# A batch's two small token tiles turned by half-row transposes in one step, and combine weights stacked four batches at a time

## The chip, the cores and the metric

The kernel runs on one core of one Trainium2 chip. The metric is the device time of one execution in microseconds (us), as the median of three runs. Beside it stands one execution that was taken with the hardware profiler; all rows below come from that execution, and their times count from the start of its span.

## What is computed

Attention with a learned position bias is followed by a soft mixture of experts. Inputs and outputs are float32.

```python
scores = q @ k.T / 8 + bias                    # B, H, S, D = 8, 8, 576, 64
attn   = softmax(scores) @ v
x      = attn.transpose(0, 2, 1, 3).reshape(4608, 512)
logits = x @ phi                               # 32 slots: 8 experts x 4
d = softmax(logits, axis=0)                    # over the 4608 tokens: dispatch
slot_input = d.T @ x                           # 32 x 512
slot_out   = relu(slot_input @ w1[e]) @ w2[e]  # per expert e, 512 -> 1024 -> 512
c = softmax(logits, axis=1)                    # over the 32 slots: combine
out = c @ slot_out                             # 4608 x 512
```

## The kernel before

The work is cut into 32 units: four pairs of heads (hp) times eight batches (b), unit u = 8 hp + b. A unit does the scores, softmax and value products of one pair of heads of one batch. Units 24 to 31 hold the last pair of heads, and each of them also does the mixture's work for its batch: `moe(u)` (line 566). A last stage then computes the slot outputs from streamed expert weights and combines them.

**The order of the work** is written out by hand in the string `ORDER` (line 24). A token `name/unit` is a step; a step emits its instructions on its engines at its place in the list, and every engine runs its own instructions strictly in that order. A `+` behind a token puts a copy on VectorE (DVE) instead of ScalarE (ACT). The steps that matter here, for a unit u and a row block p of its scores:

- `Sp.n` (line 417) computes scores on TensorE (PE) into two PSUM banks, `tp.hn` (line 442) adds the bias on DVE and thereby reads one of these banks, `ep.h` is the exponential on ACT, `mp` the reciprocal of the sums on DVE, `np.h` the scaling on GpSimd.
- `Tp`, `Rp` (lines 481, 515) turn the scaled rows by `half_turn` (line 403): one transpose of 64 rows by 128 columns, so that two row halves r = 0, 1 go to two different banks. `cp`, `cRp` (lines 501, 521) copy them out.
- `M0`, `M1`, `Mr` are the value products; `x0`, `x1` (line 556) copy their two banks into the token tile `xts`.
- `K01`, `K23`, `KR` (lines 592, 604) turn the tokens, `kc01`, `kc23`, `krc` copy them out; `L` (line 620) computes logits, `lc` copies them; `D` sums them over head groups; `d1`, `d2`, `dq`, `d3` (lines 649 to 706) take minima (DVE), exponentials into the tile `et2` (ACT), a copy of the logits into the tile `lq`, and the running state.
- `W` (line 720) turns `et2`, the dispatch weights, and `C` (line 731) turns `lq`, the combine logits: each by one 128 x 128 transpose and one of 32 x 128 (lines 712, 713), into one PSUM bank each. `wc` (line 723) copies the first into `ek`. `cA` (line 734) reads the second bank twice on DVE (a minimum over 32 slots, line 737, and a subtraction, line 738); `cB` and `cC` finish the softmax over slots in the tile `ck`. The last unit, 31, turns other tiles (line 716).
- `Z` (line 755) multiplies `ek` with the turned tokens on PE, `zc` (line 776) adds the result to a running sum on DVE.
- `A0`, `A1` (`stack`, line 1013) put the combine weights of four batches each into a pair of banks by 20 matmuls against an identity, and `Ac0`, `Ac1` (`stacked`, line 1027) copy them out. In the list they stand among the last steps of unit 31.

Then come `turn_slots` (line 974, its transpose is line 978), `first(j)` (line 986), the first expert product for j = 0 to 7, and the rest of the last stage; `refetch` issues the loads of later weights into tiles that `first(j)` has read.

**PSUM** has eight banks. `Banks(w, n)` (line 371) takes one bank or an aligned pair when a step is emitted, always the one that has been idle longest, and gives it back after the n-th `read()`:

```python
if w == 2:
    self.k = 2 * min((max(idle[2 * k], idle[2 * k + 1]), k) for k in range(4)
                     if 2 * k in idle and 2 * k + 1 in idle)[1]
```

So which earlier readers a step must wait for follows from the list alone. `T`, `R`, `K`, `L` and `Z` take pairs; `S` and `M0` take two single banks each.

Of the kernel before, what the change touches and what calls it, by code (L numbers as in the profile page):

```python
# [48 lines left out]
t1.11/2 S3.0/2+ t3.00/2 t3.10/2 lv/2 S2.0/2+ t2.10/2 e0.0/2 m0/2 n0.1/2 t2.00/2 S3.1/2+ t3.01/2 e1.0/2 t3.11/2 e1.1/2 w0/8 M0/1
S2.1/2+ S4.0/2 M1/1 m1/2 e3.0/2 t2.11/2 n0.0/2 t2.01/2 t4.10/2 e3.1/2 m3/2 e2.1/2 e2.0/2 t4.00/2 S4.1/2 t4.11/2 e4.1/2 m2/2 n1.1/2  # L50
n1.0/2 Mr/1 t4.01/2 x0/1 n3.0/2 n3.1/2 T3/2 e4.0/2 lv/3 x1/1+ R1/2 cR1/2 c3/2+ T0/2 c0/2 m4/2 S1.0/3 n2.1/2 t1.10/3 T1/2 n2.0/2
t1.00/3 c1/2 S1.1/3 n4.0/2 t1.11/3 T2/2 t1.01/3 c2/2 n4.1/2 e1.1/3 S0.0/3 S2.0/3 R3/2 t0.00/3 w1/10 t0.10/3 cR3/2+ T4/2 R4/2 cR4/2
t2.10/3 c4/2 t2.00/3 xs/1 S0.1/3+ e1.0/3 t0.01/3 t0.11/3 S3.0/3+ e0.1/3 e0.0/3 S2.1/3+ S3.1/3+ t2.11/3 e2.1/3 m1/3 t2.01/3 e2.0/3
xs/0 t3.10/3 n1.0/3 t3.00/3 M0/2 M1/2 n1.1/3 t3.11/3 m0/3 n0.1/3 t3.01/3 Mr/2 e3.0/3 m2/3 e3.1/3 x0/2 n0.0/3 R1/3 x1/2 cR1/3+ T0/3
m3/3 n2.1/3 n2.0/3 c0/3 lq/4 S1.0/4 T1/3 S1.1/4 t1.00/4 T2/3 t1.10/4 t1.11/4 c1/3 n3.0/3 t1.01/4 c2/3 S2.0/4 t2.10/4 t2.00/4
n3.1/3 T3/3 R3/3 cR3/3+ S0.0/4+ c3/3 e1.0/4 lq/5 S2.1/4+ lv/4 t0.10/4 e1.1/4 t0.00/4 S0.1/4+ t0.11/4 t0.01/4 m1/4 t2.11/4 e0.1/4
t2.01/4 S3.0/4+ t3.00/4 n1.0/4 t3.10/4 M0/3 e0.0/4 m0/4 n1.1/4 S4.0/4 S3.1/4+ t3.01/4 e2.1/4 e2.0/4 xs/2 e3.0/4 t3.11/4 m2/4
e3.1/4 M1/3 S4.1/4 t4.10/4 t4.11/4 e4.1/4 n0.1/4 Mr/3 t4.00/4 t4.01/4 x1/3 n2.1/4 m3/4 x0/3+ e4.0/4 n2.0/4 S1.0/5+ n0.0/4 R1/4
lv/5 cR1/4 t1.00/5 t1.10/5 T0/4 c0/4 S1.1/5 m4/4 t1.01/5 T1/4 n3.0/4 n3.1/4 c1/4 T2/4 t1.11/5 c2/4+ T3/4 c3/4 S0.0/5 n4.1/4 n4.0/4
T4/4 t0.00/5 R3/4 cR3/4 t0.10/5 S2.0/5 R4/4 cR4/4+ S3.0/5+ S0.1/5+ c4/4 M0/4 t2.10/5 t2.00/5 t3.10/5 S2.1/5+ t0.01/5 e1.0/5  # L60
# [155 lines left out]
def body(ctx, tc, qk, v, phi, mw1, mw2, tabh, consth, *outs):  # L216
# [349 lines left out]
    def moe(u):  # L566
# [138 lines left out]

        step(u, "d3", state)

        def turned(src, src2):
            h = Banks(1)
            pe = h.t  # L710
            if not fin:
# [467 lines left out]
```

## Time and profile before

| what | value |
|---|---|
| median of 3 runs | 539.65 us (539.45 to 541.40) |
| the profiled execution | 539.52 us, of which the span is 537.7 us |
| PE busy | 518.5 us, 96% of the span |
| DVE busy | 429.8 us, 80% |
| ACT busy | 459.1 us, 85% |
| GpSimd (POOL) busy | 223.2 us, 42% |
| DMA, mean over the span | 205 GB/s |

PE is TensorE's matmul stream and PEld its weight loads, which overlap it. A row of the timeline gives the start, the length, the engine, the line and operation, output <- inputs and a count; in brackets the idle time of the engine ahead of it and the instruction that ended this. Instructions of a helper carry the helper's line: 406 is `half_turn`, 360 every plain copy. In the chain of waits, a piece is a stretch in which one engine set the end of the program.

### The profile page before, as it was taken

To read this page: it belongs to the slowest core of one execution; us is meant where nothing else is said; L and a number is where in the kernel's file an instruction comes from. 1 tells how busy PE (TensorE), PEld (TensorE's weight loads), DVE (VectorE), ACT (ScalarE), POOL (GpSimd) and SP (SyncE) were. 2 spreads that over 40 slices of the span, in tenths; PEclk is the share of its full clock that TensorE was granted. 3 is DMA by queue.
4 is the path that set the end of the run, shared out by engine and by line. 5 is a ranking of instruction groups with operands and counts; after the bars stand their busy time and mean duration, and the time that the engine had idled before them with its cause. 6 is when DMAs were issued, how large, how long until landed. Compare 5 with 4: busy or idle time off the path is not lost.

```text
span 537.7 us, 22777 instructions
## 1 busy us (share of the span) xinstructions
PE 518.5 (96%) x9087; PEld 349.8 (65%) x9087; DVE 429.8 (80%) x1803; ACT 459.1 (85%) x988; POOL 223.2 (42%) x317
## 2 busy tenths in 40 slices
PE   8999899999989999999999999999999999999894
PEld 6444566767767676686776667666777667663661
DVE  6989878889879888889888888988899888761243
ACT  7998999999989999999999999999898898751132
POOL 4300655555454556565455556545234342300000
PEclk9999999999999999999999999999999999999997
DMA  6699535163963545576254638635632546999988
GB/s 217 245 313 351 169 108 196 47 209 115 281 190 117 189 129 173 172 243 221 68 188 138 211 129 260 171 115 195 231 98 69 172 130 219 322 354 378 406 324 328
DMA packets 40793, 110.14 MB, mean 205 GB/s; under 512 B 5360, under 2 KB 5488, under 8 KB 40688
## 3 DMA queue, kind: packets, MB, share of 16 engines
q1 hardware_dynamic: 40688, 108.70, 59.2%
q8 instruction: 71, 1.16, 0.9%
q14 instruction: 34, 0.28, 0.2%
HBM read 81.28 MB, written 27.41 MB: 202 GB/s over the span
## 4 chain that ended last, share of the span: by engine, by line
PE 81%; ACT 5%; DVE 5%; DMA 4%; issue 2%; POOL 1%; DVEq 0%; SPq 0%; ACTq 0%; POOLq 0%
PE ps L549 24%; PE ps L406 17%; PE ps L431 14%; PE ps L425 11%; PE ps L1041 3%; PE ps L993 3%; PE ps L1071 2%; PE ps L913 2%; DMA v<-in_v_dram 2%; DMA bias_m<-e 2%; DVE f L900 2%; PE ps L624 1%; ACT y L462 1%; DVE y L451 1%; ACT f L898 1%
## 5 line engine op out<-in xcount | busy, mean ns | idle before, releaser
L357 POOL TENSOR_SCALAR y<-y,rc 128x576 f32<-128x576 f32 x288 | 211.1, 750 | 219.1 <-DVE rc L470 171.6
L462 ACT ACTIVATE y<-y,mn 128x576 f32<-128x576 f32 x288 | 221.0, 776 | 7.9 <-DVE mn L451 6.8
L549 PE MATMUL ps<-at,v 64*64 64x288 f32 x2304 | 152.2, 403 | 2.1 <-DMA v<-in_v_dram 2.1
L360 ACT COPY at<-ps 128x1024 f32<-128x1024 f32 (+3 forms) x197 | 141.0, 759 | 10.3 <-PE ps L406 7.4
L451 DVE CUSTOM_DVE_ANT_0 y<-ps,bm 128x320 f32<-128x320 f32 x256 | 115.5, 487 | 10.5 <-PE ps L425 3.9
L549 PEld LDWEIGHTS ps<-at,v 64*64 64x64 f32 x2304 | 89.7, 133 | 49.2 <-DVE rc L470 2.7
L406 PEld LDWEIGHTS ps<-ident,y 64*128 64x128 f32 x2592 | 98.7, 138 | 32.8 <-POOL y L357 12.8
L451 DVE CUSTOM_DVE_ANT_0 y<-ps,bm,mn 128x256 f32<-128x256 f32 x256 | 113.9, 479 | 6.2 <-PE ps L425 1.1
L406 PE MATMUL ps<-ident,y 64*128 64x64 f32 x2592 | 106.6, 224 | 1.5 <-DVE mn L451 0.9
L431 PE MATMUL ps<-qk 64*64 64x256 f32 (+1 forms) x1280 | 92.9, 407 | 0.1
L425 PE MATMUL ps<-qk 64*128 64x320 f32 (+1 forms) x512 | 86.7, 431 | 1.3 <-DVE mn L451 1.2
L431 PEld LDWEIGHTS ps<-qk 64*64 64x64 f32 x1280 | 45.2, 132 | 28.7 <-ACT at L360 6.9
L462 ACT ACTIVATION_READ_ACCUMULATOR y<-y,mn 128x1 f32 x288 | 56.7, 197 | 0.0
L451 DVE DVE_READ_ACCUMULATOR2_ANT mn<- 128x1 f32 x576 | 48.3, 84 | 0.0
L425 PEld LDWEIGHTS ps<-qk 64*128 64x128 f32 x512 | 42.5, 189 | 7.3 <-DVE mn L451 3.0
L900 DVE TENSOR_SCALAR f<-tabw,offs 128x512 f32<-128x512 f32 (+17 forms) x107 | 39.9, 454 | 1.5 <-DMA bias_m<-e 1.4
L360 DVE COPY at<-ps 128x256 f32<-128x256 f32 (+3 forms) x59 | 34.5, 595 | 7.4 <-PE ps L406 6.4
L913 PE MATMUL ps<-f,wbd 128*32 128x512 f32 (+48 forms) x640 | 39.4, 390 | 0.5 <-ACT e L926 0.4
L913 PEld LDWEIGHTS ps<-f,wbd 128*32 128x32 f32 x640 | 18.3, 110 | 22.3 <-issue 10.2
L469 DVE TENSOR_REDUCE rc<-sm 128x2 f32<-128x4 f32 x144 | 22.0, 153 | 10.2 <-ACT y L462 9.8
L926 ACT ACTIVATE e<-ps,cons 128x591 f32<-128x591 f32 x35 | 26.7, 821 | 1.9 <-PE ps L913 1.9
L470 DVE RECIPROCAL rc<-rc 128x2 f32<-128x2 f32 x144 | 23.9, 166 | 5.0
(146 smaller groups left out, 404.6 us busy)
## 6 DMA issues: line engine op xcount, KB each, us to landing
wt<-in_moe_w_dram SPq DMA_DIRECT2D x62, 512.0 KB, 6.3
qk<-in_qk_dram SPq DMA_DIRECT2D x32, 576.0 KB, 4.1
bias_m<-e SPq DMA_DIRECT2D x32, 295.5 KB, 3.8
v<-in_v_dram SPq DMA_DIRECT2D x32, 288.0 KB, 3.3
bm<-bias_m SPq DMA_DIRECT2D x32, 288.0 KB, 4.9
out_dram<-ob SPq DMA_DIRECT2D x16, 512.0 KB, 4.5
xs<-xts SPq DMA_DIRECT2D x24, 288.0 KB, 4.3
xo<-xs SPq DMA_DIRECT2D x8, 864.0 KB, 4.7
```

The costliest lines, as they stand in the source:

```text
L357: nc.gpsimd.tensor_scalar(out=out, in0=y, scalar1=r, scalar2=1.0, op0=ALU.mult, op1=ALU.mult)
L360: (nc.vector.tensor_copy if eng else nc.scalar.copy)(out=out, in_=in_)
L406: nc.tensor.matmul(out, src[rs], ident[rs, rs], is_transpose=True, start=True, stop=True, tile_position=(64 * r, 0))
L425: nc.tensor.matmul(pss[hh].t[:, 0:nk], x[rs, S + p * P:S + (p + 1) * P], x[rs, ks], start=True, stop=True, tile_position=(64 * hh, 0))
L431: nc.tensor.matmul(pss[hh].t[64 * r:64 * r + 64, 0:nk], x[rs, q0:q0 + 64], x[rs, ks], start=True, stop=True, tile_position=(64 * hh, 64 * r))
L451: nc.vector.tensor_tensor_reduce(out=heads(hh)[:, cuts[n] // 64:cuts[n + 1] // 64], in0=d["ps", p, n][hh].read()[:, 0:nk].rearrange("a (k ...
L462: nc.scalar.activation(out=y, in_=y, func=AF.Exp, bias=d["mn", p][:, 2 + hh:3 + hh], scale=-1.0, accum_out=d["sm", p][:, hh, 0:1])
L470: nc.vector.reciprocal(out=r, in_=r)
L549: nc.tensor.matmul(d["po"][c].t[o:o + 64, 0:HALF], d["v"][rs, 64 * k:64 * k + 64], at[rs, c, 320 * k + start[c]:320 * k + start[c] + HALF] ...
L900: nc.vector.tensor_scalar(out=f, in0=tabw[:, 0:n], scalar1=off, scalar2=0.0, op0=ALU.add, op1=ALU.max)
L913: nc.tensor.matmul(x[32 * t:32 * t + 32, a:a + c1 - c0], wbd, y, start=True, stop=True, tile_position=(0, 32 * t))
L926: nc.scalar.activation(out=out, in_=x, func=AF.Copy, scale=invs[:, i:i + 1])
```

## The change

For units 24 to 30, `W` and `C` become one step, `W`: it takes a pair of banks and turns both tiles by eight half-row transposes; `wc` copies its part (now 192 elements wide, with 32 that nobody reads) and `cA` reads the other part, now by one minimum over six groups and two subtractions. The pair is given back after both readers. Unit 31 keeps its two steps.

`ck` is laid out so that the weights of four batches lie side by side, and `stack` turns them by nine half-row transposes in place of 20 matmuls. `stack` is called after the whole list, ahead of `turn_slots`, and `stacked` after `first(0)`. The host's reading of the output follows the new layout.

```diff
-    ck = const.tile([P, B, 5, 32], F32, name="ck")
+    ck = const.tile([P, 2, 5, 4, 32], F32, name="ck")
...
+        def both_turned(_):
+
+            h = m["W"] = m["C"] = Banks(2, 2)
+            for i, x in enumerate((et2, m["lq"])):
+                for j in range(2):
+                    for r in range(2):
+                        half_turn(h.t[:, r, 128 * i + 64 * j:128 * i + 64 * j + 64], x[:, P * j:P * j + P], r)
...
+            ek = xp.tile([P, 6, 32], F32, name="ek", tag="ek", bufs=2)
+            cp(eng, ek.rearrange("a (r c) s -> a r (c s)", r=2), x[:, :, 0:96])
+            m["ek"] = _Picked(ek, (0, 1, 3, 4, 2))
...
-        step(u, "W", weights)
+        step(u, "W", weights if fin else both_turned)
...
+            pk = x[:, :, 128:224].rearrange("a r (c s) -> a r c s", c=3)
+            km2 = km.rearrange("a (r c) -> a r c", r=2)
+            nc.vector.tensor_reduce(out=km2, in_=pk, axis=AX.X, op=ALU.min)
+            nc.vector.tensor_tensor(out=c_[:, 0:4].rearrange("a (r c) s -> a r c s", r=2), in0=pk[:, :, 0:2],
+                                    in1=km2[:, :, 0:2].unsqueeze(3).to_broadcast([P, 2, 2, 32]), op=ALU.subtract)
+            nc.vector.tensor_tensor(out=c_[:, 4:5], in0=pk[:, 0, 2:3], in1=km2[:, 0, 2:3].unsqueeze(2).to_broadcast([P, 1, 32]),
+                                    op=ALU.subtract)
...
-        step(u, "C", combine)
+        if fin:
+            step(u, "C", combine)
...
-        for i in range(4):
-            for j in range(4):
-                nc.tensor.matmul(h.t[32 * j:32 * j + 32, 0, i * P:(i + 1) * P], ck[:, 4 * q + i, j], ident, start=True,
-                                 stop=True, tile_position=(0, 32 * j))
...
+        for j in range(5):
+            for r in range(2 if j < 4 else 1):
+                half_turn(h.t[:, r, 64 * j:64 * j + 64], ck[:, q, j].rearrange("a b s -> a (b s)"), r)
...
             f()
+        stack(0)
+        stack(1)
         turn_slots()
         for j in range(4):
             first(j)
+            if j == 0:
+                stacked(0)
+                stacked(1)
```

In the order list only `W`, `wc`, `C`, `cA`, `A` and `Ac` move. The stretches, before and after (steps of other units between them are cut):

```
24 before: x0/25 T0/26 T1/26 n4.1/26 m2/26 cR1/26+ x1/25+ c1/26+ n4.0/26 W/24 e1.0/27 n2.0/26 C/24 cA/24 c0/26 L/25 wc/24 Z/24
24 after:  x0/25 T0/26 W/24 wc/24 cA/24 T1/26 n4.1/26 m2/26 cR1/26+ x1/25+ c1/26+ n4.0/26 e1.0/27 n2.0/26 c0/26 L/25 Z/24
25 before: x0/26 W/25 wc/25+ ... R1/27 w0/23 x1/26+ cR1/27+ n2.0/27 T1/27 c1/27 S0.0/28 ... m3/27 t0.00/28; far behind: C/25 ... cA/25
25 after:  x0/26 ... R1/27 W/25 wc/25+ cA/25 w0/23 x1/26+ cR1/27+ n2.0/27 T1/27 c1/27 S0.0/28 ... m3/27 t0.00/28
26 before: x0/27 n1.0/28 C/26 w0/21 ... W/26 e3.1/28 wc/26 ... t0.00/29 R1/28 cR1/28 T0/28 cA/26 cB/26 m3/28 ... t0.10/29 c0/28 S0.1/29
26 after:  x0/27 n1.0/28 w0/21 ... e3.1/28 ... t0.00/29 R1/28 W/26 wc/26 cR1/28 T0/28 cA/26 cB/26 m3/28 ... t0.10/29 c0/28 S0.1/29
27 before: d3/27 KR/27 lv/30 T1/29 n3.1/29 W/27 wc/27+ S4.0/30 S4.1/30 krc/27 Z/27; far behind: C/27 dq/28+ e1.0/30 cA/27
27 after:  d3/27 KR/27 lv/30 W/27 cA/27 T1/29 n3.1/29 wc/27+ S4.0/30 S4.1/30 krc/27 Z/27
28 before: W/28 wc/28 lc/29+ R1/30 cR1/30 lv/31 T1/30 D/29 C/28 c1/30 ... dq/29 ... d1/29 Z/28 cA/28
28 after:  lc/29+ R1/30 W/28 wc/28 cR1/30 lv/31 T1/30 D/29 c1/30 ... dq/29 ... d1/29 Z/28 cA/28
29 before: d2/29 W/29 zc/28 wc/29 ... K01/29 kc01/29 d3/29 KR/29 krc/29+ T2/30 c2/30 S1.1/31; far behind: C/29 ... D/30 cA/29
29 after:  d2/29 zc/28 ... K01/29 W/29 wc/29 cA/29 kc01/29 d3/29 KR/29 krc/29+ T2/30 c2/30 S1.1/31
30 before: M0/31 M1/31 Mr/31 J1/30 x1/31 W/30 kc23/30+ ... L/31 ... C/30 ... D/31 wc/30+ Z/30 dq/31 cA/30
30 after:  W/30 M0/31 M1/31 Mr/31 J1/30 x1/31 kc23/30+ ... L/31 ... D/31 wc/30+ Z/30 dq/31 cA/30
31 before: F2/30 F3/30 kc23/31 A0/31 krc/31 Z/31 zc/31 wxt/31 wxo/31 A1/31 Ac0/31 wxk/31 Ac1/31
31 after:  F2/30 F3/30 kc23/31 krc/31 Z/31 zc/31 wxt/31 wxo/31 wxk/31
```

## Rows read from the trace of the kernel before

**Rows 1.** The chain that ended last, by engine, share of the span.

```profile
PE 81%; ACT 5%; DVE 5%; DMA 4%; issue 2%; POOL 1%; DVEq 0%; SPq 0%; ACTq 0%; POOLq 0%
```

**Rows 2.** Stretches: length, busy PE PEld DVE ACT POOL, PEclk, DMA share, GB/s.

```profile
400.00:410.00 10.00, 9.97 (x172) 6.85 (x166) 9.41 (x44) 8.77 (x27) 5.74 (x8) 1.00 0.52 172
508.00:510.00 2.00, 0.67 (x16) 0.22 (x6) 0.00 (x0) 0.00 (x0) 0.00 (x0) 1.00 1.00 395
```

**Rows 3.** Pieces of the chain of waits: start, length, what.

```profile
374.48 0.26 PE ps L712
374.73 0.18 PE ps L713
...
437.15 0.32 DVE ck L738
...
464.97 0.26 PE ps L712
```

**Rows 4.** Timeline of the weight loads, half-row transposes R1/26, T0/26, T1/26.

```profile
373.14 1.20 PEld L406 LDWEIGHTS ps<-ident,y 64*128 64x128 f32 x36 [0.44 <-issue]
```

**Rows 5.** Groups by line and shape from 400 us on: count, busy us, mean ns, idle.

```profile
L738 DVE TENSOR_TENSOR ck<-ps,km 128x160 f32<-128x160 f32 x7 | 2.3, 325 | 0.2
...
L737 DVE TENSOR_REDUCE km<-ps 128x5 f32<-128x160 f32 x6 | 1.9, 317 | 0.0
```

**Rows 6.** Timeline around unit 29's d1: dq's copy on ACT, minima on DVE.

```profile
446.05 0.32 ACT L360 COPY lq<-ps 128x192 f32<-128x192 f32 x1
...
446.40 0.42 DVE L660 TENSOR_REDUCE mb<-ps 128x1 f32<-128x128 f32 x2 [1.05 <-ACT lq L360]
```

**Rows 7.** Timeline around unit 24's W: x0/25, x1/25, c1/26, L/25.

```profile
373.26 0.40 ACT L360 COPY xts<-ps 128x288 f32<-128x288 f32 x1 [0.44 <-PE ps L549]
...
373.86 0.45 DVE L360 COPY xts<-ps 128x288 f32<-128x288 f32 x1
...
374.59 1.23 DVE L360 COPY at<-ps 128x1024 f32<-128x1024 f32 x1 [0.27 <-PE ps L406]
...
375.27 0.12 PEld L624 LDWEIGHTS ps<-xo,phis 128*32 128x32 f32 x3
```

**Rows 8.** Timeline around unit 25's W: x1/26 on DVE, S0.0/28 and S0.1/28.

```profile
390.81 0.45 DVE L360 COPY xts<-ps 128x288 f32<-128x288 f32 x1
...
390.91 1.19 PE L425 MATMUL ps<-qk 64*128 64x320 f32 x8
```

**Rows 9.** Timeline around unit 26's W: wc/26, S0.1/29, t0.10/29.

```profile
407.64 0.27 ACT L360 COPY ek<-ps 128x160 f32<-128x160 f32 x1
...
407.99 0.68 PE L425 MATMUL ps<-qk 64*128 64x256 f32 x4
...
408.38 0.47 DVE L451 CUSTOM_DVE_ANT_0 y<-ps,bm 128x320 f32<-128x320 f32 x1
```

**Rows 10.** Timeline around unit 27's W: wc/27 and Z/27.

```profile
424.07 0.31 DVE L360 COPY ek<-ps 128x160 f32<-128x160 f32 x1
...
425.01 0.61 PEld L762 LDWEIGHTS ps<-xk,ek 128*32 128x32 f32 x16 [0.39 <-issue]
```

**Rows 11.** Timeline, units 28 to 31: lc/29, R1/30 with T1/30, krc/29, S0.1/31.

```profile
443.91 0.76 DVE L360 COPY lp<-ps 128x576 f32<-128x576 f32 x1 [0.21 <-PE ps L624]
...
444.21 0.70 PEld L406 LDWEIGHTS ps<-ident,y 64*128 64x128 f32 x20
...
449.45 1.40 DVE L360 COPY xk<-ps 128x512 f32<-128x512 f32 x2
...
450.90 0.70 PE L425 MATMUL ps<-qk 64*128 64x256 f32 x4
```

**Rows 12.** Timeline at the list's end: ACT's kc23/31 and krc/31.

```profile
478.39 2.11 ACT L360 COPY xk<-ps 128x1024 f32<-128x1024 f32 x3
```

**Rows 13.** Chain of waits at the list's end: A1, right ahead of turn_slots.

```profile
481.13 0.87 PE ps L1021 x32
482.00 0.26 PE ps L1024 x8
```

More of the change, by code (lines that the diff above doesn't have):

```diff
@@ L181 @@
[L181 to L184 removed]
+f12.2/-1 f15.0/-1 f9.2/-1 f15.3/-1+ f15.2/-1 f15.1/-1 B15/-1 f9.1/-1+ f12.1/-1+ f13.3/-1 f11.0/-1+ f13.0/-1 f11.2/-1
+f13.2/-1+ f11.3/-1+ f13.1/-1 f6.0/-1 f2.1/-1+ E15/-1 f11.1/-1 B13/-1 f12.3/-1+ f7.0/-1 B11/-1 f12.0/-1 B12/-1 f7.2/-1+
@@ L706, in moe, with turned @@
         step(u, "d3", state)
-        def turned(src, src2):
+        def turned(src):
             h = Banks(1)
-            pe = h.t
-            if not fin:
-                nc.tensor.transpose(out=pe[:, 0:P], in_=src2[:, 0:P], identity=ident)
-                nc.tensor.transpose(out=pe[:, P:P + 32], in_=src2[0:32, P:2 * P], identity=ident[0:32, 0:32])
-            else:
-                for cc in range(5):
-                    nc.tensor.transpose(out=pe[:, 32 * cc:32 * cc + 32], in_=src[0:32, cc * P:(cc + 1) * P],
-                                        identity=ident[0:32, 0:32])
-            return h
@@ L720, in weights @@
-        def weights(_):
-            m["W"] = turned(et, et2)
-        def keep_weights(eng):
-            m["ek"] = xp.tile([P, 5, 32], F32, name="ek", tag="ek", bufs=2)
-            cp(eng, m["ek"], m["W"].read()[:, 0:160].rearrange("a (c s) -> a c s", c=5))
-        step(u, "W", weights)
+            for cc in range(5):
+                nc.tensor.transpose(out=h.t[:, 32 * cc:32 * cc + 32], in_=src[0:32, cc * P:(cc + 1) * P],
+                                    identity=ident[0:32, 0:32])
+            return h
@@ L1018, in stack @@
         h = ends["H", q] = Banks(2)
-        for i in range(4):
-            for j in range(4):
-                nc.tensor.matmul(h.t[32 * j:32 * j + 32, 0, i * P:(i + 1) * P], ck[:, 4 * q + i, j], ident, start=True,
-                                 stop=True, tile_position=(0, 32 * j))
-        for i in range(4):
-            nc.tensor.matmul(h.t[32 * i:32 * i + 32, 1, 0:P], ck[:, 4 * q + i, 4, :], ident, start=True, stop=True,
-                             tile_position=(0, 32 * i))
+        for j in range(5):
+            for r in range(2 if j < 4 else 1):
+                half_turn(h.t[:, r, 64 * j:64 * j + 64], ck[:, q, j].rearrange("a b s -> a (b s)"), r)
     def stacked(q):
         h = ends["H", q].read()
-        nc.vector.tensor_copy(out=ends["cT", q], in_=h[:, 0].rearrange("a (b n) -> a b n", n=P))
-        nc.scalar.copy(out=ends["cR"][:, q], in_=h[:, 1, 0:64])
+        nc.vector.tensor_copy(out=ends["cT", q].rearrange("a j (r n) -> a r j n", r=2),
+                              in_=h[:, :, 0:256].rearrange("a r (j n) -> a r j n", j=4))
+        nc.scalar.copy(out=ends["cR"][:, q], in_=h[:, 0, 256:320])
     def second(k, Q, parts=(0, 1)):
@@ L1092, in body @@
     homes2 += [(wp, "w", (1024,)), (wp, "w", (1024,)), (wp, "w", (512,))]
-    for q in range(2):
-        step(U - 1, f"A{q}", lambda _, q=q: stack(q))
-        step(U - 1, f"Ac{q}", lambda _, q=q: stacked(q))
     with tc.manual_schedule():
@@ L1173 @@
     o = np.empty((8, 576, 512), np.float32)
-    o[:, 0:512] = main.reshape(4, 2, 2, 128, 2, 4, 128).transpose(1, 5, 2, 4, 6, 0, 3).reshape(8, 512, 512)
+    o[:, 0:512] = main.reshape(4, 2, 2, 128, 2, 4, 128).transpose(1, 2, 4, 5, 6, 0, 3).reshape(8, 512, 512)
     o[:, 512:] = rest.reshape(4, 128, 4, 2, 64).transpose(3, 2, 4, 0, 1).reshape(8, 64, 512)
```

361 lines of the change are left out of this document (195 added, 166 removed).

## Prediction

> **What bounds the kernel now.** I read the chain of waits first, then the busy time by stretch, then the timeline around each step that moves. The chain is PE for 81% of the span [rows 1]: look for a stretch in which PE never rests. In the mixture's stretch PE is busy 9.97 of 10 us and DVE 9.41 [rows 2]. DVE is a step behind PE, so work taken from PE pays only while DVE still hands back PSUM banks in time. Late in the last stage the picture turns: from 508 to 510 us PE is busy 0.67 of 2 us while the DMA share is 1.00 [rows 2]. [...]
>
> **The turns.** In each of seven batches a full transpose costs the chain 0.26 us and the small one 0.18, and both come twice: 0.88 us (the first two of four such pieces stand in [rows 3]). Half-row transposes come at 1.20/36 = 0.033 us each [rows 4], so eight cost 0.27 and a batch saves 0.61 us of PE, 4.3 us over seven. [...]
>
> **What is added.** `wc` copies 192 values in place of 160, about 0.03 us more. `cA` was 0.317 + 0.325 us [rows 5]. Its minimum now covers 192 values, between 0.32 and 0.38 (in proportion); the subtraction becomes two, together between 0.33 and 0.65. I take 0.35 + 0.50 = 0.85, in the middle, so 0.2 more on DVE in each batch. More important, two engines do not read one bank at the same time here: unit 29's minima on DVE need nothing from dq's copy but waited until it had ended at 446.37, and began at 446.40 [rows 6]. So `cA` also waits for `wc` where `wc` is on ACT and listed first (units 24, 26, 28, 29).
>
> **The pairs.** The new step holds a pair until both readers are done. I followed `Banks` through both lists, as the list alone fixes who takes which bank. The waits that this changes are the main cost.
>
> Unit 24: only one pair is idle when W/24 is emitted, and T1/26, the very next PE step, must take the same pair back. T0's last load ends at 373.14 + 20 x 0.033 = 373.8; x0/25 has freed the pair at 373.66 [rows 7]. W's loads end at 374.07. In the trace 0.25 us lie between the last load of T1 (374.34) and the start of its copy (374.59) [rows 4, 7], so `wc` starts at 374.3, `cA` at 374.65 and ends at 375.5. T1 started at 373.8 before and now at 375.5; its 16 loads end at 376.05. L/25, which started at 375.27 [rows 7], follows: 0.8 late with the saved turns already counted. It also needs x1/25, which ran at 373.86 on DVE and is now queued behind `cA`, behind m2/26 and cR1/26. PE holds L/25 and Z/24 behind it, ACT holds e1.0/27 and c0/26 behind `wc`. Bounds +0.7 (T1 alone, a shorter `cA`) and +1.3 (x1 late as well); I take **+1.0**.
>
> Unit 25: `cA` now stands ahead of x1/26 on DVE, which moves from 390.81 to 391.67 and ends at 392.1 [rows 8]. The second bank of S0.0/28 is now the one that x1/26 frees. S0.0 and S0.1 ran from 390.91 to 392.10, that bank's part from about 391.2. So PE loses some 0.75, and gains 0.44 when C/25 is not met later: **+0.3**, bounds 0 and +0.5.
>
> Unit 26: the second bank of S0.1/29 becomes the one that t0.10/29 frees, which stands behind `cA` and m3/28 on DVE. wc/26 ends near 407.95, `cA` at 408.8, then t0.10 takes 0.47: free between 409.3 and 409.5 [rows 9]. S0.1 ended at 408.67 and would now end near 409.7: **+1.0**, bounds +0.6 and +1.2. The saving is inside, as PE only waits longer.
>
> Unit 27: cA/27 moves ahead of wc/27, which goes from 424.07 to 424.9 [rows 10]. S4.1/30 takes `wc`'s bank for both halves, and Z/27 comes behind: about 0.7 late of 425.01. But `cA` leaves a place where DVE was the chain: 0.32 at 437 [rows 3] and most of the 0.317 of its minimum. **+0.1**, bounds -0.3 and +0.4.
>
> Units 28 and 29: T1/30 now takes lc/29's pair, free at 443.91 + 0.76 = 444.67, and ran from 444.35 (behind R1's four loads) [rows 11]: 0.3 late, and so D, dq and d1 of unit 29. On DVE come 0.2 more for cA/28 and 0.85 for cA/29, both ahead of krc/29. That moves from 449.45 by 1.35. S0.1/31 takes krc's banks and already started right at its end (450.85, started 450.90) [rows 11]. **+1.2**, bounds +0.6 and +1.4. Later C/29 leaves the chain: **-0.4**, the last piece of [rows 3] with the small one behind it.
>
> Unit 30: C/30 and W/30 stood where L/31 and D/31 waited for copies, so nothing is saved; W/30 is put ahead of M0/31, where PE has no gap: 0 to 0.27, I take **+0.2**.
>
> **The stacks.** A0 goes at no gain: Z/31 waits for krc/31, which ends at 478.39 + 2.11 = 480.50 on ACT [rows 12], and that covers it. A1 lies on the chain with 0.87 + 0.26 us [rows 13]; in its place come 18 half-row transposes, 0.59, partly beside zc/31. Bounds -0.4 and -1.1; I take **-0.6**. `stacked` costs nothing: its copies fall under first(1) to first(3), where DVE and ACT have no other work; without that cover they would be four copies on the path. Its banks go back before first(4) needs a new pair. The moved steps issue no DMA. GpSimd's memset of `lq` waits for the turn that read it and can only come earlier; the weight loads that SP issued between A0 and Ac1 wait for other tiles.
>
> **Sum.** 1.0 + 0.3 + 1.0 + 0.1 + 1.2 - 0.4 + 0.2 - 0.6 = +2.8 at first(0). The weights run at full DMA share behind it [rows 2], and their loads start as units 30 and 31 give up tiles, about +3.6 late by these terms; DMA was the later of the two at 508 us, so the end lies between +2.8 and +3.6. I keep +2.8, since PE reaches the weights earlier in this sum than the loads' shift says and the DMA gaps before can take the rest. On the profiled execution's own 539.52 us (span 537.7 and 1.8 around it) that is 542.3; the median of the runs lies 0.13 higher: 542.4.
>
> **Rivals.** First, faster: PE stays the bound and the pairs are there in time. [...] From rows: units 24 to 26 save 0.61 each, W/27 and W/28 0.17 each, C/29 0.4, the stacks 0.6, against 0.2 for W/30 and 0.3 for a longer `cA`: -2.5, 537.1 us. For it speaks PE's 81% [rows 1]; against it DVE's 9.41 of 10. The place that decides is T1/26: below about 0.6 us of wait there, the turn pays. Chance 0.20. Second, about half of the stalls: DVE and ACT work ahead while PE waits at unit 24, so units 25 and 28 to 29 lose little: +1.0, 540.6; chance 0.22. Third, the stalls add up and the weights' start carries the +3.6 and more to the end: +4, 543.6; chance 0.13. The forecast has 0.45. That the step itself fails to be shorter is hardly open, as rows 4 are the same instruction in the same alternation of halves.
>
> **Numbers.** 0.5%, 2.7 us, is about what a measurement of this kernel can tell from no change: the bounds are 536.9 and 542.4. The forecast has its middle at the upper one, so half of it, 0.23, and nearly all of the third rival, 0.13, are slower; a little of the second adds 0.01. Of the first rival under half is faster, 0.09. That leaves 0.54. The range of 537.3 to 543.9 leaves out half of the first rival and a third of the third, and some of the forecast's upper edge. The forecast's own range, with its bounds, is 541.2 to 543.6.
>
> **What would show it.** Right: an idle of PE or PEld of about 1.3 us before T1/26, ended by DVE `ck`; S0.0/28 ended by DVE `xts`; S0.1/29 and S0.1/31 ended by DVE; eight loads in 0.27 us at each turn; first(0) about 2.8 us later. Wrong: T1/26 without a wait, or a first(0) that comes no later than before.

## The result and the profile after

The changed kernel takes 547.44 us (median of 6 runs, 544.82 to 550.59), the kernel before 539.55 us (6 runs beside them, 538.22 to 541.40). The ratio is 1.0149 with a 95% interval of 1.0120 to 1.0177: 7.9 us slower. 542.4 was forecast, with a range up to 543.9; the direction was right, the size wrong.

The profiled execution took 549.96 us with a span of 548.2. Its page, part 1, and the chain of waits by engine, which answers to [rows 1]:

```profile
PE 522.4 (95%) x9053; PEld 353.3 (64%) x9053; DVE 431.2 (79%) x1810; ACT 459.1 (84%) x988; POOL 217.0 (40%) x317
...
PE 77%; ACT 7%; DVE 6%; DMA 5%; issue 3%; POOL 0%; SPq 0%; DVEq 0%; ACTq 0%; POOLq 0%
```

Every engine did nearly as much as before, but PE's share of the chain fell from 81% to 77%: it waits. Where, I read from landmarks that both kernels have, the starts of `L` in units 24 to 31 and of first(0). Their absolute times are of little use, since L/24, ahead of all that is changed, already started anywhere from 359.8 to 365.8 us in the profiles of this study. The stretches between them are very good: with the stacks alone changed, seven of eight repeat those of before within 0.01 us. So a stretch says what its unit costs, to a few hundredths, in one profile, where the granted clock is 1.00 in it and PE does not stand without a reason that the profile shows. Stretches of before, and the difference from them in each profile (us):

| stretch | before | changed | changed, again | stacks alone | W/30 old place | old turns, new order | units 25-29 | places | bank kept | units 26, 30 | halves |
|---|---|---|---|---|---|---|---|---|---|---|---|
| L/24-L/25 | 12.65 | +0.90 | +0.90 | -0.01 | +0.90 | +0.98 | -0.01 | -0.63 | +0.91 | -0.01 | -0.63 |
| L/25-L/26 | 17.74 | +1.32 | +5.39 | 0.00 | +2.59 | +1.18 | +1.17 | +0.60 | +2.32 | +0.01 | +0.15 |
| L/26-L/27 | 18.18 | +2.74 | +1.18 | +0.01 | +1.18 | +0.69 | +1.18 | +0.29 | +1.17 | +1.54 | +0.42 |
| L/27-L/28 | 19.40 | +0.72 | +0.73 | -0.01 | +0.73 | +0.58 | +0.73 | +0.70 | +0.73 | 0.00 | -0.01 |
| L/28-L/29 | 12.07 | -0.57 | -0.58 | -0.01 | -0.58 | -0.57 | -0.57 | +1.06 | -0.59 | -0.02 | 0.00 |
| L/29-L/30 | 19.20 | +0.83 | +0.82 | -0.01 | +0.84 | +0.72 | +0.83 | -0.86 | +0.83 | -0.01 | 0.00 |
| L/30-L/31 | 9.37 | +3.17 | +3.08 | +0.01 | +1.71 | +3.61 | +1.61 | +1.32 | +0.12 | +1.69 | +0.01 |
| L/31-first(0) | 11.60 | -0.27 | -0.28 | -0.49 | -0.49 | -0.28 | -0.49 | +0.96 | -0.50 | -0.29 | -0.49 |
| sum | 120.21 | +8.84 | +11.24 | -0.51 | +6.88 | +6.91 | +4.45 | +3.44 | +4.99 | +2.91 | -0.55 |

From first(0) to the end of the span it was 54.9 us before, 54.5 and 54.1 in the changed kernel: the end follows first(0). (In the other profiles it was 54.0 to 55.1, and 56.6 with the stacks alone.)

**Unit 24** in the changed kernel's timeline (the lines of [rows 4, 7]):

```profile
375.73 0.20 PEld L432 LDWEIGHTS ps<-ident,et 64*128 64x128 f32 x4
...
375.85 0.21 PEld L432 LDWEIGHTS ps<-ident,lq 64*128 64x128 f32 x4
...
376.24 0.32 ACT L386 COPY ek<-ps 128x192 f32<-128x192 f32 x1 [0.61 <-PE ps L432]
...
376.59 0.36 DVE L779 TENSOR_REDUCE km<-ps 128x6 f32<-128x192 f32 x1 [1.27 <-ACT ek L386]
376.99 0.29 DVE L780 TENSOR_TENSOR ck<-ps,km 128x128 f32<-128x128 f32 x1
...
377.19 0.18 DVE L782 TENSOR_TENSOR ck<-ps,km 128x32 f32<-128x32 f32 x1
...
377.52 0.71 PE L432 MATMUL ps<-ident,y 64*128 64x64 f32 x16 [1.32 <-DVE rc L495]
```

Read downwards, it is one pair of banks passing from hand to hand: eight half-row transposes in 0.33 us, `wc` on ACT, only then `cA` on DVE (idle 1.27 us, ended by `ek`), only then T1/26, which has stood for 1.32 us. (The releaser named there, `rc`, is the DVE instruction right behind `ck`.)

**Unit 26**, where two PE steps wait ([rows 9]):

```profile
411.63 0.71 PE L432 MATMUL ps<-ident,y 64*128 64x64 f32 x15 [0.50 <-DVE mn L477]
411.94 0.36 DVE L779 TENSOR_REDUCE km<-ps 128x6 f32<-128x192 f32 x1 [0.36 <-ACT ek L386]
...
413.43 0.48 PE L451 MATMUL ps<-qk 64*128 64x256 f32 x1 [0.67 <-DVE mn L477]
```

The second is S0.1/29, held by t0.10/29 behind `cA`, as forecast (with 0.67 us in place of 1.0). The first, T0/28, was not in the forecast: its pair is now one that t0.00/29 frees. Behind them the granted clock, in stretches of 1 us (columns as in [rows 2]):

```profile
413.00:414.00 1.00, 0.57 (x8) 0.46 (x9) 0.78 (x4) 0.99 (x2) 0.82 (x2) 1.00 0.00 0
414.00:415.00 1.00, 1.00 (x23) 1.00 (x22) 0.49 (x2) 0.02 (x1) 0.64 (x1) 0.53 0.06 16
415.00:416.00 1.00, 1.00 (x16) 1.00 (x14) 0.17 (x1) 1.00 (x2) 0.00 (x0) 0.50 0.00 0
416.00:417.00 1.00, 1.00 (x7) 0.99 (x6) 1.00 (x2) 1.00 (x3) 0.00 (x0) 0.50 0.00 0
```

0.50 is the lowest granted clock in this profile. PE works without a pause there, but slowly: from 415 to 417 us the 64 x 256 score matmuls took 683 ns each, against 393 ns between 396 and 412 us, at a clock of 1.00. That is 1.56 us of this stretch's +2.74; a second profile, with the clock at 1.00 here, has +1.18.

**Unit 30**, the largest loss, in the chain of waits and then by 1 us:

```profile
472.93 0.85 ACT at L386
473.78 0.06 issue
473.84 0.33 ACT lq L386
474.17 0.02 issue
474.20 0.43 DVE mb L686 x2
474.63 0.02 issue
474.65 0.17 DVE mb L688
474.82 0.02 issue
474.85 0.47 ACT et L702 x2
475.32 0.04 issue
475.36 0.28 PE ps L432 x2
...
476.24 5.86 PE ps L575 x72
```

```profile
474.00:475.00 1.00, 0.12 (x4) 0.00 (x0) 0.73 (x5) 0.81 (x4) 0.00 (x0) 1.00 1.03 339
475.00:476.00 1.00, 0.62 (x8) 0.48 (x8) 0.90 (x6) 0.69 (x5) 0.00 (x0) 0.75 1.04 401
476.00:477.00 1.00, 1.00 (x14) 0.60 (x14) 0.96 (x5) 0.00 (x0) 0.00 (x0) 0.50 0.97 347
477.00:478.00 1.00, 1.00 (x12) 0.49 (x8) 0.50 (x1) 0.00 (x0) 0.00 (x0) 0.50 1.06 405
```

The turn of W/30 reads `et2`, which d2/30 writes on ACT, at the end of a chain of five small steps; M0/31 stands behind it. The wait in the timeline:

```profile
475.36 0.66 PE L432 MATMUL ps<-ident,et 64*128 64x64 f32 x4 [1.24 <-ACT et L702]
```

In the kernel before M0/31 did not wait for that chain at all:

```profile
466.12 2.17 PE L549 MATMUL ps<-at,v 64*64 64x288 f32 x32
...
467.31 0.31 ACT L676 ACTIVATE et<-ps,mb 128x64 f32<-128x64 f32 x1
```

It ran from 466.12, 1.5 us before `et2` was complete. And in the changed kernel PE goes on at a granted clock of 0.50 right behind the wait: its 64 x 288 value products took 694 ns each from 476.3 to 478.5 us, against 407 in the kernel before from 466.2 to 468.5, and all 72 of them 5.93 us, against 4.59.

### The profile page after: what moved, and what is told of

Its sections match the earlier page's. It is cut to its first block, busy times and chain, and to the rows that moved or that the text cites. A ratio compares the mean times of both kernels' runs of the same rounds, so it can differ in the third digit from the quotient of the medians.

```text
span 548.2 us, 22722 instructions
## 1 busy us (share of the span) xinstructions
PE 522.4 (95%) x9053; PEld 353.3 (64%) x9053; DVE 431.2 (79%) x1810; ACT 459.1 (84%) x988; POOL 217.0 (40%) x317
## 4 chain that ended last, share of the span: by engine, by line
PE 77%; ACT 7%; DVE 6%; DMA 5%; issue 3%; POOL 0%; SPq 0%; DVEq 0%; ACTq 0%; POOLq 0%
PE ps L575 24%; PE ps L432 16%; PE ps L457 13%; PE ps L451 11%; PE ps L1084 3%; DMA bias_m<-e 3%; PE ps L1039 3%; PE ps L1114 2%; ACT y L488 2%; PE ps L650 2%; DVE y L477 2%; DMA v<-in_v_dram 2%; ACT e L972 1%; PE ps L279 1%; DVE f L946 1%
## 5 line engine op out<-in xcount | busy, mean ns | idle before, releaser
L575 PE MATMUL ps<-at,v 64*64 64x288 f32 x2304 | 153.8, 406 | 0.5 <-DMA v<-in_v_dram 0.5
L432 PEld LDWEIGHTS ps<-ident,y 64*128 64x128 f32 x2592 | 101.3, 139 | 38.2 <-POOL y L383 13.2
L575 PEld LDWEIGHTS ps<-at,v 64*64 64x64 f32 x2304 | 91.8, 134 | 47.0 <-ACT at L386 1.2
L432 PE MATMUL ps<-ident,y 64*128 64x64 f32 x2592 | 110.3, 226 | 4.5 <-DVE rc L495 1.8
L451 PE MATMUL ps<-qk 64*128 64x320 f32 (+1 forms) x512 | 89.2, 436 | 2.6 <-DVE mn L477 1.9
L451 PEld LDWEIGHTS ps<-qk 64*128 64x128 f32 x512 | 44.0, 191 | 9.4 <-DVE mn L477 3.9
```

The source lines that it names most:

```text
L432: nc.tensor.matmul(out, src[rs], ident[rs, rs], is_transpose=True, start=True, stop=True, tile_position=(64 * r, 0))
L451: nc.tensor.matmul(pss[hh].t[:, 0:nk], x[rs, S + p * P:S + (p + 1) * P], x[rs, ks], start=True, stop=True, tile_position=(64 * hh, 0))
L575: nc.tensor.matmul(d["po"][c].t[o:o + 64, 0:HALF], d["v"][rs, 64 * k:64 * k + 64], at[rs, c, 320 * k + start[c]:320 * k + start[c] + HALF] ...
```

## The experiments

There were eleven more runs: ten other kernels, and the changed one once more. Each is given against the kernel before in the same session, and by its column in the table above; where there is no column, the stretches are named. Of a kernel's edits, only the lines that matter are shown.

### The stacks alone

```diff
+JOINT = set()
...
-        step(u, "W", weights if fin else both_turned)
+        step(u, "W", both_turned if joint else weights)
...
-        if fin:
+        if not joint:
             step(u, "C", combine)
```

`joint` is true for the units in `JOINT`, here none. It runs with the turns and the order of the kernel before; `ck`, `stack` and `stacked` stay changed.

> The kernel before with the stacks alone changed (weights laid out by four batches, nine half-row transposes each, called behind the list); W and C as before, in their old places. If the stacks are the small gain that the changed kernel's trace shows between L/31 and first(0) (-0.27 us), all of L/25 to L/31 stand as before and the time is about 539.2 us, 0.3 below the kernel before. Rival: the weights' loads set the end and nothing changes, 539.5 us. Second rival: the stacks are part of the loss, because copies under the first expert products collide there; then 540.5 us or more.

540.23 us, ratio 1.0012 (0.9988 to 1.0037): no difference that can be measured. In the profile first(0) comes 0.51 earlier, all of it behind L/31. The stacks are a small gain and no part of the loss; the seven zeros of this column are what makes the table readable to a few hundredths. The gain does not reach the end of this profile, where it is 56.6 us from first(0) on in place of 54.9. PE waits there for nothing that the profile shows from 506.69 to 508.01, and then runs three microseconds at a granted clock of 0.50:

```profile
509.00:512.00 3.00, 3.00 (x58) 2.68 (x60) 1.22 (x1) 0.75 (x1) 0.00 (x0) 0.50 0.69 270
```

### W/30 back in its old place

```diff
-W/30 M0/31 M1/31 Mr/31 J1/30 x1/31 kc23/30+
+M0/31 M1/31 Mr/31 J1/30 x1/31 W/30 kc23/30+
```

> The changed kernel with W/30 alone put back behind x1/31, where it stood before; still one joint step. Theory: in its new place W/30 makes PE wait for the exponentials of d2/30 on ACT ahead of M0/31, and this wait is most of the +3.2 us between L/30 and L/31. Then that stretch falls back to within 0.7 us of before and the time to about 544.7 us. Rival: the stretch is long because ACT and DVE come late out of the earlier units; then it stays at +2.5 us or more and the time at 547 us.

545.60 us, ratio 1.0112 (1.0058 to 1.0166). L/30 to L/31 falls from 3.17 to 1.71 over before, so with the rest of the kernel as changed W/30's place is 1.4 of it; neither theory had the 1.7 that stay (the experiment with a bank kept says what they are). The clock tells what the 1.4 are: in this stretch 0.86 in both profiles of the changed kernel, and here

```profile
464.74:475.82 11.08, 9.75 (x183) 6.13 (x175) 5.68 (x17) 6.00 (x16) 1.49 (x3) 1.00 0.94 337
```

### The old turns in the new order

```diff
-x0/25 T0/26 W/24 wc/24 cA/24 T1/26
+x0/25 T0/26 W/24 C/24 wc/24 cA/24 T1/26
```

and so in all seven units; `W` and `C` are the old full turns into one bank each.

> The changed kernel's order of steps, with C right behind W, but the old turns (a full transpose and a small one each) into one bank each, given back after one reader. Theory one, the shared pair is the cause: T1/26 finds its pair at once, L/25 comes within 0.3 us of before, and L/27 within 1.5 us; the time is about 542 us, what is left being W/30's wait of about 2. Theory two, the order is the cause, because wc and cA now stand ahead of work of other units on ACT and DVE: L/25 is 0.5 us or more late, L/27 3.5 us or more, and the time 546 us or more.

546.75 us, ratio 1.0125 (1.0093 to 1.0156), first(0) +6.9. The time and L/25 (+0.98) are those of theory two, the order; L/27, with 0.98 + 1.18 + 0.69 = 2.85, lies between its 3.5 and the 1.5 of theory one. And its reason is not quite the one given. At unit 24 the list leaves one idle pair. W and C, as single banks, break it up, so T1/26 must wait for `cA` here as well: this run does not part the shared pair from the place at unit 24. At unit 26 the stretch pays 0.69 in place of 1.18. There W/26 waits for x1/27, and no other PE step by more than 0.3 us, where the changed kernel has the two waits of 0.50 and 0.67:

```profile
411.12 0.33 PE L741 MATMUL ps<-ident,et 128*128 128x128 f32 x1 [0.63 <-DVE xts L388]
```

The stretch of unit 30 again has a clock of 0.87.

### Units 25 to 29 only

```diff
+JOINT = {25, 26, 27, 28, 29}
...
-        step(u, "W", weights if fin else both_turned)
+        step(u, "W", both_turned if joint else weights)
```

Units 24 and 30 stand in the list as before, the others as changed.

> The changed kernel with units 24 and 30 put back to separate turns in their old places; the joint step in units 25 to 29 only. Theory one, the lateness of ACT and DVE after unit 24's stall is carried on into units 25 and 26: without it L/27 comes about +2.0 us late in place of +5.0 (so less than the 0.9 of unit 24 alone would explain), and the time is about 541.5 us. Theory two, each unit pays its own wait whatever went before: L/27 at +4.1 us and the time 547.4 - 0.9 - 3.2 = 543.3 us.

543.52 us, ratio 1.0069 (1.0042 to 1.0096). The time is theory two's. L/24 to L/27 loses 2.34, between the 2.0 of theory one and the 4.1 of theory two; but the 4.1 had in it the 1.56 us of lowered clock of the first profile, and 2.5 are left without them. Stretch by stretch it is plain: 1.17 and 1.18 here, and 1.32 and, at a clock of 1.00, 1.18 where unit 24 is stalled as well. Each unit pays its own wait. L/30 to L/31 still loses 1.61, with unit 30 as before: the first sign that its place is not the whole cause.

### The changed kernel once more

> The changed kernel once more, for a second profile. Where the granted clock fell in the first (0.92 of full speed between L/26 and L/27, 0.86 between L/30 and L/31) two theories differ. If the fall follows from this kernel's own waits, both stretches are again some 1.5 us longer than the waits alone make them (20.9 and 12.5 us) with the clock at about 0.9. If it is chance of one execution, the clock is 1.00 there and the stretches are 19.4 and about 11.1 us.

One execution, 551.92 us. Between L/30 and L/31 the clock is 0.86 again and the stretch 12.45: the fall came in both executions, as the first theory has it. Between L/26 and L/27 the clock is 1.00 and the stretch 19.36, as the second has it: the first fall there belonged to that execution. A new stall stands between L/25 and L/26:

```profile
385.80 0.80 PE L432 MATMUL ps<-ident,y 64*128 64x64 f32 x11 [2.62 <-issue]
```

with the clock at 0.93 behind it. "Issue" means that PE waited for nothing that the profile shows. The same stall, behind the same sixth load of the same sixteen, is there with W/30 in its old place (1.25 us) and with the bank kept (next, 0.97 us), not in the first profile.

### A bank kept from C/29 to D/30

```diff
-T2/31 c2/31 D/30 dq/30
+T2/31 G/29 c2/31 D/30 g/29 dq/30
+        if u == 29:
+            step(u, "G", lambda _: m.update(G=Banks(1)))
+            step(u, "g", lambda _: m["G"].read())
```

W/30 is in its old place too.

> The changed kernel with W/30 in its old place, and in addition one PSUM bank is taken where C/29 stood and given back behind D/30, with no instruction in between. With that M0/31 finds the two banks of c2/31, as in the kernel before, in place of one that d2/30 reads last. Theory: the +1.7 us that are left between L/30 and L/31 with W/30 in its old place are M0/31's wait for d2/30 through this bank, a consequence of C/29 having left; they go, and C/29's saved turn shows: that stretch is at -0.4 us against before (9.0 us), the time about 543.5 us. Rival: ACT and DVE come late into this stretch (cA/29 and krc/29 moved) and M0/31 would wait anyway; then it stays above 10.5 us.

544.50 us, ratio 1.0116 (1.0076 to 1.0156). L/30 to L/31 falls from +1.71 to +0.12:

```profile
467.38:476.87 9.49, 9.07 (x183) 5.96 (x175) 5.67 (x17) 5.98 (x16) 1.48 (x3) 1.00 0.98 341
```

No instruction was added. A bank that C/29 used to hold had steered M0/31 to the two banks of c2/31; without C/29 it gets D/30's, and waits for d2/30. That is shown for W/30 in its old place. The saved turn of C/29 (-0.4) did not appear on top. In the kernel before, C/29's turn ran at 464.90 while the next PE step, R3/31, had to wait for a pair that a DVE copy frees; without C/29 PE rests there instead. Before, and with the bank kept:

```profile
464.58 1.23 DVE L360 COPY at<-ps 128x1024 f32<-128x1024 f32 x1 [1.61 <-PE ps L406]
464.90 0.33 PE L712 MATMUL ps<-ident,lq 128*128 128x128 f32 x1
...
465.86 0.34 PE L406 MATMUL ps<-ident,y 64*128 64x64 f32 x4
```

```profile
471.37 0.34 PE L433 MATMUL ps<-ident,y 64*128 64x64 f32 x4 [0.42 <-DVE at L387]
```

### Units 26 and 30 only

```diff
+JOINT = {26, 30}
```

> The kernel before with the stacks, and the joint step in its new place in units 26 and 30 alone; the other units as before. Two questions, read from two stretches. Unit 26: if the units price their waits one by one, L/26 to L/27 pays the +1.2 us that it paid with units 25 to 29 changed, less the 0.4 that C/25, back in its old place, costs there either way: +1.2 to +1.6 us. If that price was lateness handed on by unit 25, it is +0.5 us or less. Unit 30: if W/30 ahead of M0/31 is enough by itself to make PE rest and the granted clock fall, L/30 to L/31 is +3 us with a granted clock near 0.86; if it takes the lateness of units 28 and 29 as well, the clock stays 1.00 and the stretch is at +1.7 us or less. Time 544 us by the first theories, 541 us by the rivals.

543.37 us, ratio 1.0056 (1.0023 to 1.0089). Unit 26 pays +1.54 with nothing late ahead of it; with C/25 still there (0.44 by the forecast, not measured alone) that is 1.1 to 1.2 net, the first theory. The waits themselves are others here: 0.51 us of W/26 for x1/27 and 0.74 of S0.1/29, none of T0/28, so the equal sum is partly chance. Unit 30 pays +1.69 with the clock at 1.00: W/30 makes PE wait 1.27 us for `et2`, but that rest alone did not bring the clock down. C/29 is in its old place in this kernel. By the list, W/30 takes the pair of c2/31 ahead of M0/31, so M0/31 gets D/30's bank here too.

```profile
462.33:473.39 11.06, 9.77 (x184) 6.32 (x177) 5.85 (x18) 5.64 (x15) 1.55 (x3) 1.00 0.91 336
```

### The joint step in roomier places

```diff
-x0/25 T0/26 W/24 wc/24 cA/24 T1/26 n4.1/26 m2/26 cR1/26+ x1/25+ c1/26+ n4.0/26 e1.0/27 n2.0/26 c0/26 L/25 Z/24
+x0/25 T0/26 T1/26 n4.1/26 m2/26 cR1/26+ x1/25+ c1/26+ n4.0/26 e1.0/27 n2.0/26 c0/26 W/24 wc/24 cA/24 L/25 Z/24
...
-R1/27 W/25 wc/25+ cA/25 w0/23 x1/26+ cR1/27+ n2.0/27 T1/27
+R1/27 w0/23 x1/26+ cR1/27+ W/25 wc/25+ cA/25 n2.0/27 T1/27
```

and alike in the other five units.

> The changed kernel's joint step and its stacks, with W, wc and cA of all seven units moved to places where the list leaves a pair idle for some time and the banks taken behind it were given back long before (unit 24: behind T1/26, ahead of L/25; 25: behind x1/26 and cR1/27; 26: behind x1/27; 27: behind x0/28; 28: ahead of S0.0/31; 29: ahead of K23/29; 30: ahead of D/31). Theory: the loss comes from the places, not from the joint step, so the waits go and PE's saving shows: L/24 to L/25 -0.6, the two stretches behind it -0.6 each, L/27 to first(0) together -1 or so; first(0) about 2.8 us earlier than before and the time near 537 us. Rival: the step itself is dear (the readers of one pair follow each other, cA is longer on DVE); then L/24 to L/27 stays at +1.5 us or more over before and the time at 541 us or more.

541.89 us, ratio 1.0028 (1.0005 to 1.0051): the theory's 537 failed. The rival's time came, but not its stretch: L/24 to L/27 is at +0.26, not at +1.5. Unit 24 gives -0.63, to a few hundredths PE's saving:

```profile
377.43 0.20 PEld L433 LDWEIGHTS ps<-ident,et 64*128 64x128 f32 x4
...
377.56 0.20 PEld L433 LDWEIGHTS ps<-ident,lq 64*128 64x128 f32 x4
...
377.83 0.12 PEld L651 LDWEIGHTS ps<-xo,phis 128*32 128x32 f32 x3
```

`L` follows 0.4 us behind the first turn and nobody waits. In the other units I chose places by how long ago the banks had been given back in the list, and that was not enough: the rest of the sum is +4.1. Of these some 1.45 are a lowered clock between L/31 and first(0) (+0.96 in place of -0.49), ahead of which PE had rested no more than in kernels without a fall there:

```profile
476.90:489.46 12.56, 11.44 (x192) 8.24 (x191) 8.98 (x34) 6.84 (x17) 0.00 (x0) 0.86 0.90 329
```

The others are waits. At unit 30, +1.32, M0/31 waits for d2/30. At unit 26 PE still stands 1.20 us, behind `x1/27` and `cA` on DVE; unit 28's step stands one stretch earlier than in the changed kernel, and the two have +1.06 and -0.86. That a bank has long been free does not say that its next reader is.

### Half-row transposes without the joint step

```diff
+            h = Banks(2)
+            for j in range(2):
+                for r in range(2):
+                    half_turn(h.t[:, r, 64 * j:64 * j + 64], src[:, P * j:P * j + P], r)
```

for W/26 and C/30 in their old places, with one reader each; unit 24 alone has the joint step.

> The kernel before with the stacks, the joint step in unit 24 alone, behind T1/26 and with wc and cA ahead of c0/26; and W/26 and C/30 by four half-row transposes into a pair of their own, given back after one reader, in their old places. Theory: half-row transposes are worth their 0.3 us (one tile) and 0.6 us (two) on PE where the pair they take was idle and nobody waits for it: L/24 to L/25 -0.6 us, L/25 to L/26 within 0.1 of before, L/26 to L/27 -0.3, first(0) about 1.4 us earlier than before, the time 538 to 539 us if the end follows first(0), 539.6 us if the loads of the expert weights set the end. Rival: a wider pair costs a later step as much as the turn saves; then first(0) is not earlier than with the stacks alone (-0.5 us).

539.67 us, ratio 1.0000 (0.9977 to 1.0023). -0.63 at unit 24 as expected, +0.15 behind it where 0.1 was the most expected; W/26 has +0.42 for the expected -0.3, and first(0) comes 0.55 earlier, not 1.4. T0/28 now takes the pair that wc/26 frees:

```profile
406.59 0.71 PE L435 MATMUL ps<-ident,y 64*128 64x64 f32 x16 [0.40 <-ACT ek L389]
```

A wider turn is itself a consumer of pairs: the rival, at this place.

### Unit 24 alone, twice

Both are the kernel before with the stacks and this one stretch of the list changed, first:

```diff
-cR1/26+ x1/25+ c1/26+ n4.0/26 W/24 e1.0/27 n2.0/26 C/24 cA/24 c0/26 L/25 wc/24 Z/24
+cR1/26+ x1/25+ W/24 wc/24+ c1/26+ n4.0/26 e1.0/27 n2.0/26 cA/24 c0/26 L/25 Z/24
```

> What the runs so far point to: the kernel before with the stacks, and the joint step in unit 24 alone, behind T1/26, with wc on DVE ahead of c1/26 and cA ahead of c0/26. L/24 to L/25 -0.6 us, the stretch behind it within 0.1 us of before (with wc on ACT, Z/24 came 0.1 late there), the others as before, L/31 to first(0) -0.5: first(0) 1.1 us earlier. If the end follows first(0), the time is 538.5 us, 0.2% below before, about as much as five rounds can tell; if the weights' loads set the end, it is no different from before. Rival: wc on DVE makes c1/26 late, and the stretch behind L/25 gives the 0.6 back.

538.39 us, ratio 0.9973 (0.9952 to 0.9994). -0.63, then +0.50, the rival: Z/24 takes the pair of c1/26, which is late on DVE behind `wc`.

```profile
376.87 1.09 PE L816 MATMUL ps<-xk,ek 128*32 128x256 f32 x16 [0.48 <-DVE at L388]
```

and second:

```diff
+cR1/26+ x1/25+ c1/26+ n4.0/26 W/24 e1.0/27 n2.0/26 wc/24 cA/24 c0/26 L/25 Z/24
```

> The kernel before with the stacks and the joint step in unit 24 alone, this time with wc on ACT, as in the run with the halves, ahead of c0/26 (there the stretch behind L/25 lost 0.15 us; with wc on DVE it lost 0.50, because c1/26, whose pair Z/24 takes, came behind wc). Expected: L/24 to L/25 -0.63, the next stretch +0.15, the others 0, L/31 to first(0) -0.49: first(0) 0.97 us earlier than before and 0.3 earlier than with wc on DVE; the time 538.2 us, 0.3% below before. Rival: the end does not follow first(0), and the time is no different from before, 539.8 us.

538.36 us, ratio 0.9961 (0.9944 to 0.9978). Every stretch came as written within 0.01 us: -0.63, +0.15, five zeros, -0.49, first(0) 0.98 earlier. It is faster than the kernel before by 0.4% (the interval is 1.2 to 3.0 us, and the stretches account for 1.0 of them), and by some 1.8% than the changed one, measured in another session (0.9961 against 1.0149). In these runs the change pays in one unit of seven, in another place than it was put, and in the stacks.

## Why the prediction was wrong, step by step

**The parts were priced right.** Eight half-row transposes take 0.33 us (0.27 forecast), and where nothing waits a batch saves 0.63 (0.61). `cA` takes 0.36 + 0.29 + 0.18 = 0.83 (0.85). `cA` waits for `wc` where both are on one pair: in the group by line its minimum has 1.6 us of idle time ended by `ek`.

**Unit 24**, +1.0: 0.90, by the mechanism named. The point from which the first rival would have won, a wait of T1/26 below 0.6, was passed with 1.32.

**Unit 25**, +0.75 up to L/26: 1.32, and 1.17 with unit 24 as before. The wait of S0.0/28 for x1/26 is there; T1/27 stands besides, since its pair now contains a bank that t1.11/28 frees late. In the kernel with units 25 to 29 only:

```profile
393.57 0.51 PEld L433 LDWEIGHTS ps<-ident,y 64*128 64x128 f32 x14 [0.20 <-DVE mn L478]
...
394.91 0.30 PEld L452 LDWEIGHTS ps<-qk 64*128 64x128 f32 x4 [0.60 <-DVE xts L387]
```

The second row is the forecast wait, the first was missed: I had looked at the banks of S0.0 only. The two rows make 0.80 of the 1.17; what the rest is, no row here tells.

**Unit 26**, +1.0, less 0.44 for C/25: 1.18 in place of 0.56. The step that failed is the same: S0.1/29's wait was priced, at 1.0 for the 0.67 measured, and T0/28's (0.50) was not seen, though it follows from the same list.

**Units 27 to 29.** Unit 27 was to be +0.1 net, some 0.7 late and most of it given back where `cA` leaves: +0.72 and -0.57. Units 28 and 29: +0.83 where 1.2 stood with a lower bound of 0.6. Right.

**"Later C/29 leaves the chain: -0.4" and "W/30 is put ahead of M0/31, where PE has no gap: 0 to 0.27"** are the largest errors of the sum: together -0.2 was forecast for the stretch from L/30 to L/31, and +3.17 came. Some 1.7 of it is one wait for d2/30, and each of the two moves brings it. C/29's going alone gives M0/31 another bank, which D/30's readers free late (+1.71 and +1.61 with W/30 in its old place, +0.12 with the bank kept). W/30 ahead of M0/31 alone needs `et2` itself and takes the pair that M0/31 had (+1.69 with C/29 in place). In the changed kernel both hold, and by the sizes the wait is paid once. I had followed the list through the banks of the steps that the change moves, but not through those of a step that only inherits; and I had asked what PE does at W/30's new place, not when its operand is ready. The -0.4 were misread from the chain: C/29's turn there only filled a wait of R3/31. The other 1.4 to 1.5 are the clock, which falls where the two come together behind the late units 28 and 29 (12.45 and 12.54 us at a clock of 0.86 against 11.08 at 1.00).

**The clock** has no term in the sum, and that failed. In the rows there is one stretch in which PE rests, in the last stage, and the granted clock is 1.00 there [rows 2]. One stretch of rest was no evidence for others: 1.4 us at unit 30 each time, 1.56 at unit 26 in one of two profiles, and with the stacks alone the clock fell to 0.50 behind the same kind of rest in the same stage. Nor does that stretch show that DMA was the later of the two: PE stands there for nothing that the profile shows.

```profile
509.58 0.14 PEld L1041 LDWEIGHTS ps<-wt,hT 128*32 128x32 f32 x2 [1.60 <-issue]
```

Falls came behind rests of 0.67 us (unit 26), 1.24 (unit 30), 1.32 (the last stage, the stacks alone) and 2.62 (the changed kernel once more), and none behind the rests of 1.3 us at unit 24. No rival of mine had a stall cost twice, as at unit 30: 1.24 us as a wait and 1.4 to 1.5 as a slow stretch behind it.

**The stacks**, -0.6: -0.49 alone, -0.28 behind the changed unit 30. **The end**, up to 0.8 behind first(0) by the weights' loads: no; from first(0) on nothing is lost, and the changed kernel's two profiles are 0.4 and 0.8 us shorter there than the one of before.

In sum at first(0): +2.8 forecast. Without the falls of the clock and the unexplained stall, the waits of the changed kernel are 0.90 + 1.32 + 1.18 + 0.73 - 0.58 + 0.82 + 1.7 - 0.3 = 5.8, with unit 30's clock 7.2, and the medians differ by 7.9; the rest may be the stalls and falls that come in some executions only; it was not measured by itself. The third rival (the stalls add up) came nearest, for a reason other than its own: not the weights' start, but each unit in full. (The first rival's own terms add up to -2.7, 537.0 us, where -2.5 stands; that changes no chance.)

## What to carry to other kernels

When a step is moved or merged under an allocator that goes by the list, compare for every later step which reader frees the bank it now gets, not for the moved ones alone: here a step that disappeared cost 1.6 us with W/30 in its old place, and one that got shorter cost 0.4, by the banks alone. Ask of a moved step both what its engine does there and when its operand is ready. Price a merged step by the latest of its readers; a saving of 0.63 us on the busiest engine paid in the one place where nobody wanted the pair back.

## What was not expected of the hardware

**The clock.** It fell between L/30 and L/31 in each profile in which PE waited for W/30 behind the late units 25 to 29 (to a mean of 0.86, 0.86 and 0.87 over the stretch), not with W/30 moved back and not in units 26 and 30 alone, where PE rested as long (1.27 us) for the same `et2`. In the three that fell, PE also rested 0.42 us for R3/31's pair just ahead of the wait of 1.2 us; in units 26 and 30 alone the turns of C/29 fill that place. Whether this decides was not tested. The rest of 1.3 us at unit 24 never brought the clock down, in four profiles, and in the last stage it fell behind one rest of 1.32 us (the stacks alone) and not behind one of 1.33 (the kernel before). So the length of one rest does not tell; what does, these runs leave open.

**A stall without a releaser**, between the sixth and seventh load of one group of sixteen: 2.62, 1.25 and 0.97 us, absent in another execution of the same program. The traces hold a trail that goes some way. One DMA queue, q8, of the kind that the page calls instruction, moves 71 packets of 16 KB in an execution, about one for every 255 matmuls and weight loads of TensorE (18,106 in the changed kernel):

```profile
q8 instruction: 71, 1.16, 0.9%
```

In the three stalled executions the last packet ahead of the stall ended at 384.33, 378.28 and 381.00, and the loads went on at 385.80, 379.71 and 382.37, 1.4 to 1.5 us behind it each time. In the one without the stall it had ended at 381.63, 1.4 us before the seventh load's turn. Two rests in the last stage fit too: packet at 508.17 and load at 509.58 in the kernel before, packet at 506.64 and matmul at 508.01 with the stacks alone. So in these five cases PE went on 1.37 to 1.47 us behind a packet of this queue. That it waited for its own instructions is my guess from these times; neither that nor why the packet came late is shown by a run here.

**Repeatability.** Between L/24 and first(0) the same program text takes the same time to 0.03 us, as long as neither of these two comes in. Most of the scatter of several us between executions lies ahead of that (L/24 at 359.8 to 365.8), some behind it (54.0 to 56.6 us from first(0) on).
